# Strided Q and K weights, one head selector, and Q weights loaded by row chunks, in a fused attention-plus-GLU block

## Chip, cores, metric

One core of one Trainium2 chip. The metric is the device time of one execution, in microseconds (us). The kernel before takes 289.22 us (median of four runs, 289.21 to 289.25).

## The reference, cut to what matters

```python
x = A_x                       # 1 x 2048 x 640
xn = _layernorm(x)
# A: attention, 32 heads of 20 features; each position sees itself and 7 positions behind it, 2 apart
qkv = (xn @ wqkv).reshape(B, S, 3, 32, 20)
logits = einsum("bhsd,bhswd->bhsw", q, k[idx]) * 20 ** -0.5     # idx = pos - 2*w, w = 0..7
o = einsum("bhsw,bhswd->bhsd", softmax(masked logits), v[idx])
# B: bilinear GLU
out = x + o @ wo + ((xn @ w_gate) * (xn @ w_up)) @ w_down
```

A head has 20 features, and the 640 features lie on 5 chunks of 128 partitions. So in the natural order some heads straddle chunks: head 6 is features 120 to 139.

## The kernel before

Every operation is recorded in program order by a small scheduler, which inserts the semaphore waits. Everything is bf16 with fp32 accumulation. The work runs in this order: layer norm of 16 row tiles, transposes, Q/K projections; Q*K products on VectorE (DVE) with logits summed per head on TensorE (PE); softmax on DVE; V windows read back from a DRAM scratch, weighted on DVE and summed on PE. The V and GLU projections and the output projection fill PE in between.

Set-up of the head selector, and the first loads:

```python
G = sb("G", [128, NCH, H])                       # one selector for each of 5 chunks
op("pool", memset(G[:], 0.0))
op("pool", affine_select(G[:], G[:], pattern=[[128, NCH], [-DH, H]], compare_op=is_gt,
                         fill=1.0, base=-(DH - 1), channel_multiplier=1))
op("pool", affine_select(G[:], G[:], pattern=[[128, NCH], [-DH, H]], compare_op=is_ge, fill=0.0, ...))
# ... (abridged calls)
def wqkv_load(g, lo=0, hi=D):
    dst = WQKV[:, g, :, lo:hi]
    dma(dst, wqkv_src[:, :, g * D + lo:g * D + hi], ...)

x_load(0)
x_load(1)
wqkv_load(0, 0, 2 * 128)        # Q, columns for output chunks 0 and 1
wqkv_load(0, 2 * 128, D)        # Q, the other columns
x_load(2)
wqkv_load(1)                    # K
for t in range(3, 8):
    x_load(t)
```

The Q/K projections come in three sizes: `proj_part` moves 128 columns of the transposed activations per matmul, `proj_wide` 256 and `proj` 512. All take their weights (the stationary operand) as

```python
l, x = WQKV[:, which, c, m * 128:(m + 1) * 128], XNT[:, c, ...]
```

and every matmul brings its own weight load (PEld in the profile). The logits:

```python
def qk_logits(batch):
    for w, c, s in batch:
        lb = 4 + w % 4
        for j in range(NJ):
            o, x = PS[32 * j:32 * j + 32, lb, :], PRD[:, s, j * JB:(j + 1) * JB]
            matmul(o, G[:, c, :], x, start=(c == 0), stop=(c == NCH - 1), tile_position=(0, 32 * j))
```

The tail adds the residual x, read a second time into XR, and those reads are queued as an item of PE's filling work, behind V windows:

```python
fill.append((0.0, lambda: [xr_load(t) for t in range(NXR)]))     # NXR = 3
add_dn(0)
# ... and, long before that item's turn:
for u in range(NVX):
    vx_load(u)                                                   # first 8 V windows
```

Of the kernel before, what the change touches and what calls it, by code (L numbers as in the profile page):

```python
# [6 lines left out]
ALU = mybir.AluOpType  # L7

S = 2048
D = 640  # L10
NCH = 5
H = 32
DH = 20
# [7 lines left out]
TS = 128  # L21
JB = 512
# [15 lines left out]
class Sched:  # L38
# [47 lines left out]
    def op(self, eng, fn, r=(), w=(), dma=False, name=""):  # L86
        X = _Op()
        X.eng, X.fn, X.name, X.dma = eng, fn, name, dma
        X.needs_tick, X.event, X.pre_know, X.idx = False, None, None, len(self.ops)
        rk = [k for a in r for k in self.keys(a)]  # L90
        wk = [k for a in w for k in self.keys(a)]
        deps = {}
        inorder = eng in ("pe", "act", "dve")
        for k in rk:
            st = self.state.get(k)
            if st is not None and st[0] is not None:
                deps[st[0].idx] = st[0]
        for k in wk:
            st = self.state.get(k)
            if st is None:  # L100
                continue
            o, rds = st
            if o is not None and not (eng == "pe" and o.eng == "pe"):
                deps[o.idx] = o
            for q in rds:
                if inorder and q.eng == eng and not q.dma:
                    continue
                deps[q.idx] = q
        last = {}
        keep = []  # L110
        for d in deps.values():
            if d.dma or d.eng == "pool":
                keep.append(d)
            else:
                b = last.get(d.eng)
                if b is None or b.idx < d.idx:
                    last[d.eng] = d
        X.deps = keep + list(last.values())
        for d in X.deps:
            if not d.dma:  # L120
                d.needs_tick = True
        for k in rk:
            st = self.state.get(k)
            if st is None:
                self.state[k] = [None, [X]]
            elif inorder and st[1] and st[1][-1].eng == eng and not st[1][-1].dma:
                st[1][-1] = X
            else:
                st[1].append(X)
        for k in wk:  # L130
            self.state[k] = [X, []]
        if dma:
            X.event = (self.nc.alloc_semaphore(f"dma{self.n_dma}"), 16)
            self.n_dma += 1
        self.ops.append(X)
        return X
# [59 lines left out]
def build_kernel(nc, A_x, A_wqkv, A_wo, B_x, B_w_gate, B_w_up, B_w_down, out):  # L196
    K = Sched(nc)
    op = K.op
# [3 lines left out]
    def sb(name, shape, dtype=BF16, at=None):  # L202
        n = mybir.dt.size(dtype)
        for s in shape[1:]:
            n *= s
        n = (n + 63) // 64 * 64
        if at is None:
            at = place[0]
            place[0] += n
        assert at + n <= 229344, (name, at + n)  # L210
        return K.sbuf(name, shape, dtype, at)
# [5 lines left out]
    XNT = sb("XNT", [128, NCH, S])  # L217
# [11 lines left out]
    WQKV = sb("WQKV", [128, 3, NCH, D], at=a_ra)  # L229
# [27 lines left out]
    EPSC = sb("EPSC", [128, 16], FP32)  # L257
    IDENT = sb("IDENT", [128, 128])
    SEL = sb("SEL", [128, 32])
    G = sb("G", [128, NCH, H])  # L260
    PS = nc.alloc_psum_tensor("PS", [128, 8, 512], FP32)
    VSL = S + PAD + 2
    vscr = nc.dram_tensor("v_scratch", [4, D, VSL], BF16, kind="Internal").ap()
# [4 lines left out]
    def dma(o, i, r=(), w=(), name="", eng="sp"):  # L268
        return op(eng, lambda e: e.dma_start(o, i), r=r, w=w, dma=True, name=name)  # L269
# [6 lines left out]
                                         fill=1.0, base=0, channel_multiplier=1),  # L276
       r=[IDENT[:]], w=[IDENT[:]], name="ident")
    op("pool", lambda e: e.memset(G[:], 0.0), w=[G[:]], name="g0")
    op("pool", lambda e: e.affine_select(G[:], G[:], pattern=[[128, NCH], [-DH, H]], compare_op=ALU.is_gt,
                                         fill=1.0, base=-(DH - 1), channel_multiplier=1),  # L280
       r=[G[:]], w=[G[:]], name="g1")
    op("pool", lambda e: e.affine_select(G[:], G[:], pattern=[[128, NCH], [-DH, H]], compare_op=ALU.is_ge,
                                         fill=0.0, base=0, channel_multiplier=1),
       r=[G[:]], w=[G[:]], name="g2")
    op("pool", lambda e: e.memset(KT[:, :, 0:PAD], 0.0), w=[KT[:, :, 0:PAD]], name="kpad")

    def x_load(t):
        dma(XST[:, t % NXS, :], xhbm[t * TS:(t + 1) * TS, :], w=[XST[:, t % NXS, :]], name=f"xld{t}")

    wqkv_src = A_wqkv.rearrange("(c p) n -> p c n", p=128)  # L290

    def wqkv_load(g, lo=0, hi=D):
        dst = WQKV[:, g, :, lo:hi]
        dma(dst, wqkv_src[:, :, g * D + lo:g * D + hi], w=[dst], name=f"ld_wqkv{g}_{lo}")

    x_load(0)
    x_load(1)
    wqkv_load(0, 0, 2 * 128)
    wqkv_load(0, 2 * 128, D)
    x_load(2)  # L300
    wqkv_load(1)
    for t in range(3, 8):
# [68 lines left out]
               r=[ZERO[:]], w=[PS[:, 5, :]], name="warm")  # L371


    bank_ring = list(range(6))

    def bank():
        b = bank_ring.pop(0)
        bank_ring.append(b)
        return b

    def proj(which, m, j):
        b = bank()
        for c in range(NCH):
            l, x = WQKV[:, which, c, m * 128:(m + 1) * 128], XNT[:, c, j * JB:(j + 1) * JB]
            op("pe", (lambda l, x, c: lambda e: e.matmul(PS[:, b, :], l, x, start=(c == 0), stop=(c == NCH - 1)))(l, x, c),  # L385
               r=[l, x], w=[PS[:, b, :]], name=f"p{which}_{m}_{j}_{c}")
        T = (QT, KT, VST)[which]
        o0 = PAD if which == 1 else 0
        o = T[:, m, o0 + j * JB:o0 + (j + 1) * JB]
        op("act", lambda e: e.activation(o, PS[:, b, :], ACT.Copy), r=[PS[:, b, :]], w=[o], name=f"pev{which}_{m}_{j}")  # L390

    def proj_part(which, t, ms, b, col):
        for m in ms:
            o = PS[:, b, col + (m - ms[0]) * TS:col + (m - ms[0] + 1) * TS]
            for c in range(NCH):
                l, x = WQKV[:, which, c, m * 128:(m + 1) * 128], XNT[:, c, t * TS:(t + 1) * TS]
                op("pe", (lambda o, l, x, c: lambda e: e.matmul(o, l, x, start=(c == 0), stop=(c == NCH - 1)))(o, l, x, c),  # L397
                   r=[l, x], w=[o], name=f"pp{which}_{m}_{t}_{c}")

    def proj_wide(which, t0, m, b, col):  # L400
        o = PS[:, b, col:col + 2 * TS]
        for c in range(NCH):
            l, x = WQKV[:, which, c, m * 128:(m + 1) * 128], XNT[:, c, t0 * TS:(t0 + 2) * TS]
            op("pe", (lambda l, x, c: lambda e: e.matmul(o, l, x, start=(c == 0), stop=(c == NCH - 1)))(l, x, c),  # L404
               r=[l, x], w=[o], name=f"pw{which}_{m}_{t0}_{c}")

# [20 lines left out]
    def slot_of(w):  # L427
        return (w + 4) % 8
# [6 lines left out]
    def qk_logits(batch):  # L435
        for w, c, s in batch:
            lb = 4 + w % 4
            for j in range(NJ):
                o, x = PS[32 * j:32 * j + 32, lb, :], PRD[:, s, j * JB:(j + 1) * JB]
                op("pe", (lambda o, x, j, c: lambda e: e.matmul(o, G[:, c, :], x, start=(c == 0), stop=(c == NCH - 1),  # L440
                                                             tile_position=(0, 32 * j)))(o, x, j, c),
                   r=[G[:, c, :], x], w=[o], name=f"lg{w}_{c}_{j}")
        for w, c, s in batch:
            if c == NCH - 1:
                lb = 4 + w % 4
                o = LOG[:, slot_of(w), :]
                op("act", (lambda o, lb: lambda e: e.activation(o, PS[:, lb, :], ACT.Copy, scale=SCALE))(o, lb),
                   r=[PS[:, lb, :]], w=[o], name=f"lgev{w}")
                if w > 0:
                    m = LOG[0:32, slot_of(w), 0:DIL * w]  # L450
                    op("pool", (lambda m: lambda e: e.memset(m, NEG))(m), w=[m], name=f"mask{w}")
# [167 lines left out]
    for t0 in (0, 2):  # L619
        bm = bank()  # L620
        for which in (0, 1):
            for t in (t0, t0 + 1):
                b = bank()
                proj_part(which, t, (0, 1), b, 0)
                if (which, t) in ((0, 0), (1, 0), (1, 1), (1, 2), (0, 3)):
                    tr()
                proj_part(which, t, (2, 3), b, 2 * TS)
                part_evac(which, t, 1, 0, 4, b, 0)
                proj_part(which, t, (4,), bm, (2 * which + t - t0) * TS)
            part_evac(which, t0, 2, 4, 1, bm, 2 * which * TS)  # L630
    v_pad()
    for t0 in (4, 6, 8, 10):
        bm = None
        for g in range(5):
# [6 lines left out]
            else:  # L641
                which, m = ((0, 0), (0, 2), None, (1, 0), (1, 2))[g]
# [15 lines left out]
    fill = []  # L658
# [131 lines left out]
```

## Time and profile before

| what | value | view |
|---|---|---|
| time | 289.22 us | median of 4 runs |
| span, PE busy | 287.3 us, 275.4 us (96%) | page, part 1 |
| Q/K weight loads | 450: 200 under 128 moving columns, 200 under 256, 50 under 512 | program, groups |
| pitch of those matmuls (start to start) | 56, 109, 220 ns (216 with every record) | chain, time divided by count |

Part 1 of the page of the kernel before (busy us, share of the span, instructions):

```profile
span 287.3 us, 4706 instructions
PE 275.4 (96%) x1968; PEld 156.7 (55%) x1986; DVE 171.4 (60%) x260; ACT 116.1 (40%) x211; POOL 2.3 (1%) x17
```

PE is the bottleneck, with about 12 us idle in all. The weight loads overlap matmuls, so their 55% is not added to PE's 96%.

The table by stretches of the kernel before. The columns are the stretch, its length, then busy us and instruction count of PE, PEld, DVE, ACT and POOL, the granted clock (the share of full TensorE clock that was let through), the DMA share and GB/s:

```profile
6.37:21.90 15.53, 13.37 (x225) 12.51 (x225) 11.27 (x37) 6.55 (x16) 0.00 (x0) 1.00 0.53 178
...
125.00:178.00 53.00, 49.42 (x368) 24.78 (x369) 48.65 (x42) 19.40 (x36) 0.00 (x0) 0.97 0.58 171
```

PE idles mainly at the start (1.6 us before the first row, 2.2 us in it), in the V stage (3.6 us of the second, where DVE is nearly as busy as PE) and in the 2.8 us after its last matmul.

The chain of work that ended last, kernel before (start us, length us, what; "x40" counts merged instructions):

```profile
3.87 6.92 DMA XST<-in_A_x_dram
10.81 0.50 DVE STATS L327
...
19.91 2.23 PE PS L397 x40
...
23.51 2.18 PE PS L404 x20
...
47.53 8.58 PE PS L385 x39
56.11 0.98 PE PS L440 x16
...
150.47 3.91 DMA XR<-in_A_x_dram
```

Dividing gives the pitches: 2.23/40 = 56 ns with 128 moving columns (L397), 2.18/20 = 109 ns with 256 (L404), 8.58/39 = 220 ns with 512 (L385). Page part 1 has 1968 matmuls but 1986 loads, so 18 matmul records are missing from this trace, one of them here. Two DMAs stand on the chain: x tile 3, landing at about 10.8 us, and the first residual loads, issued at 150.5 us.

Weight loads of the kernel before, grouped with shapes kept apart (count, busy us, mean ns of one, idle before them):

```profile
L404 PEld LDWEIGHTS PS<-XNT,WQKV 128*128 128x128 bf16 x200 | 19.1, 98 | 2.0
L397 PEld LDWEIGHTS PS<-XNT,WQKV 128*128 128x128 bf16 x200 | 11.4, 98 | 1.8 <-DVE XNT L366 1.0 <-ACT KT L412 0.9
L440 PEld LDWEIGHTS PS<-PRD,G 128*32 128x32 bf16 x160 | 3.3, 95 | 6.4 <-DVE PRD L432 2.1 <-issue 1.7 <-ACT VST L390 0.4
L370 PEld LDWEIGHTS PS<-ZERO 128*128 128x128 bf16 x12 | 1.4, 129 | 3.3 <-issue 2.0 <-DVE EPSC L273 1.3
```

A record of one load lasts 98 ns, yet the matmuls follow each other every 56 ns: loads are pipelined, and a record's length is not the time for which it blocks the next. The twelve warm-up matmuls (L370) use one and the same tile and still have twelve loads.

### The profile page before, as it was taken

Reading aid. Unit: us, or ns where it says so; the run is one execution under the profiler, and the core shown is the slowest. Engines: PE = TensorE matmul, PEld = TensorE weight load, DVE = VectorE, ACT = ScalarE, POOL = GpSimd, SP = SyncE. Lnnn points to the kernel's source line nnn. Section 1 sums busy time; section 2 is a strip of 40 time slices with the busy share of each in tenths; the row PEclk is TensorE's granted clock in tenths of the full one; section 3 lists DMA queues with packets and bytes.
Section 4 is the critical chain, followed back from the end, with each engine's and each line's share of the span. In section 5 each row is a group of like instructions: output and inputs, shape, how many; then the busy total and the mean of one; then the engine's idle time right before and its main releaser. Section 6 shows DMA issues by size and latency. Waiting matters only on the chain.

```text
span 287.3 us, 4706 instructions
## 1 busy us (share of the span) xinstructions
PE 275.4 (96%) x1968; PEld 156.7 (55%) x1986; DVE 171.4 (60%) x260; ACT 116.1 (40%) x211; POOL 2.3 (1%) x17
## 2 busy tenths in 40 slices
PE   7899999999999999998997999999999999999996
PEld 3789887443434344443453564444676444677774
DVE  5776792999999768859994999521222112222221
ACT  2355556544644479525732034655200555300000
POOL 2000000000000000000000000000000000000000
PEclk9999999999999999999999799999999999999999
DMA  6824999007989692035976731000021100012211
GB/s 199 281 72 66 396 389 256 3 2 302 392 335 391 217 356 65 0 76 140 307 221 190 208 105 50 2 0 0 2 91 48 46 0 0 2 63 73 74 43 46
DMA packets 30468, 39.57 MB, mean 138 GB/s; under 512 B 4464, under 2 KB 26608, under 8 KB 30448
## 3 DMA queue, kind: packets, MB, share of 16 engines
q1 hardware_dynamic: 30448, 39.29, 41.5%
q8 instruction: 15, 0.25, 0.3%
q14 instruction: 5, 0.04, 0.0%
HBM read 25.07 MB, written 13.16 MB: 133 GB/s over the span
## 4 chain that ended last, share of the span: by engine, by line
PE 72%; DVE 15%; DMA 4%; issue 4%; ACT 2%; SPq 2%; DVEq 0%; ACTq 0%
PE PS L550 27%; PE PS L576 19%; PE PS L385 11%; PE PS L404 7%; PE PS L440 3%; DVE PC L510 3%; DVE PB L510 3%; DMA XST<-in_A_x_dram 2%; PE PS L397 2%; DVE PA L510 2%; SPq L269 2%; DVE SM L455 2%; DMA XR<-in_A_x_dram 1%; PE PS L360 1%; DVE RS L468 1%
## 5 line engine op out<-in xcount | busy, mean ns | idle before, releaser
L550 PE MATMUL PS<-XNT,WU 128*128 128x512 bf16 x238 | 59.4, 379 | 1.4 <-ACT USX L552 1.2
L576 PE MATMUL PS<-WD,HT 128*128 128x320 bf16 x384 | 59.0, 304 | 0.0
L550 PE MATMUL PS<-XNT,WG 128*128 128x512 bf16 x229 | 57.5, 379 | 0.7 <-issue 0.5
L432 DVE TENSOR_TENSOR PRD<-QT,KT 128x2048 bf16<-128x2048 bf16 x40 | 45.8, 1220 | 5.0 <-ACT KT L390 4.2
L576 PEld LDWEIGHTS PS<-WD,HT 128*128 128x128 bf16 x384 | 37.8, 99 | 17.2 <-issue 1.7
L552 ACT ACTIVATE HT<-PS 128x512 bf16<-128x512 f32 x48 | 29.1, 605 | 39.6 <-PE PS L550 39.6
L580 DVE TENSOR_TENSOR FOUT<-PS,XR 128x320 bf16<-128x320 f32 x32 | 15.4, 490 | 46.2 <-PE PS L576 42.5
L555 DVE TENSOR_TENSOR HT<-HT,USX 128x512 bf16<-128x512 bf16 x48 | 19.1, 420 | 39.5 <-ACT USX L552 39.5
L550 PEld LDWEIGHTS PS<-XNT,WU 128*128 128x128 bf16 x240 | 23.3, 98 | 30.1 <-ACT USX L552 1.7
L552 ACT ACTIVATE USX<-PS 128x512 bf16<-128x512 f32 x48 | 28.9, 603 | 26.3 <-PE PS L550 18.3
L550 PEld LDWEIGHTS PS<-XNT,WG 128*128 128x128 bf16 x240 | 22.9, 98 | 29.5 <-issue 1.7
L385 PE MATMUL PS<-XNT,WQKV 128*128 128x512 bf16 x145 | 32.8, 379 | 0.4 <-issue 0.3
L576 PE MATMUL PS<-WO,OT 128*128 128x320 bf16 x160 | 27.1, 300 | 0.0
L385 PEld LDWEIGHTS PS<-XNT,WQKV 128*128 128x128 bf16 x150 | 14.1, 98 | 18.8 <-ACT VST L390 2.1
L404 PE MATMUL PS<-XNT,WQKV 128*128 128x256 bf16 x200 | 23.6, 273 | 0.0
L404 PEld LDWEIGHTS PS<-XNT,WQKV 128*128 128x128 bf16 x200 | 19.1, 98 | 2.0
L527 ACT ACTIVATE OT<-PS 128x512 bf16<-128x512 f32 x20 | 11.1, 600 | 22.3 <-PE PS L520 22.1
L576 PEld LDWEIGHTS PS<-WO,OT 128*128 128x128 bf16 x160 | 15.8, 99 | 6.3
L510 DVE TENSOR_TENSOR PA<-VX,ATX 128x4096 bf16<-128x4096 bf16 x7 | 16.0, 2285 | 4.0 <-DMA ATX<-LOG 4.0
L390 ACT ACTIVATE VST<-PS 128x512 bf16<-128x512 f32 x20 | 12.0, 599 | 14.3 <-PE PS L385 14.3
L510 DVE TENSOR_TENSOR PB<-VX,ATX 128x4096 bf16<-128x4096 bf16 x7 | 16.0, 2285 | 0.2 <-PE PS L520 0.2
L510 DVE TENSOR_TENSOR PC<-VX,ATX 128x4096 bf16<-128x4096 bf16 x6 | 13.7, 2285 | 0.2 <-PE PS L520 0.2
(52 smaller groups left out, 166.5 us busy)
## 6 DMA issues: line engine op xcount, KB each, us to landing
VX<-v_scratch SPq DMA_DIRECT2D x20, 520.0 KB, 5.0
v_scratch<-VST SPq DMA_DIRECT2D x20, 512.0 KB, 4.5
XST<-in_A_x_dram SPq DMA_DIRECT2D x16, 160.0 KB, 4.6
XR<-in_A_x_dram SPq DMA_DIRECT2D x16, 160.0 KB, 2.4
out_dram<-FOUT SPq DMA_DIRECT2D x16, 160.0 KB, 1.8
WG<-in_B_w_gate_dram SPq DMA_DIRECT2D x1, 1920.0 KB, 12.0
WU<-in_B_w_up_dram SPq DMA_DIRECT2D x1, 1920.0 KB, 16.4
WD<-in_B_w_down_dram SPq DMA_DIRECT2D x1, 1920.0 KB, 22.6
```

What stands on the lines that cost most here:

```text
L385: op("pe", (lambda l, x, c: lambda e: e.matmul(PS[:, b, :], l, x, start=(c == 0), stop=(c == NCH - 1)))(l, x, c), r=[l, x], w=[PS[:, b, :] ...
L390: op("act", lambda e: e.activation(o, PS[:, b, :], ACT.Copy), r=[PS[:, b, :]], w=[o], name=f"pev{which}_{m}_{j}")
L404: op("pe", (lambda l, x, c: lambda e: e.matmul(o, l, x, start=(c == 0), stop=(c == NCH - 1)))(l, x, c), r=[l, x], w=[o], name=f"pw{which}_ ...
L432: op("dve", lambda e: e.tensor_tensor(PRD[:, s, :], QT[:, c, :], k, ALU.mult), r=[QT[:, c, :], k], w=[PRD[:, s, :]], name=f"prod{w}_{c}")
L440: op("pe", (lambda o, x, j, c: lambda e: e.matmul(o, G[:, c, :], x, start=(c == 0), stop=(c == NCH - 1), tile_position=(0, 32 * j)))(o, x, ...
L510: op("dve", lambda e: e.tensor_tensor(p[:], vw, a, ALU.mult), r=[v, at], w=[p[:]], name=f"pv{u}")
L527: op("act", (lambda o, b: lambda e: e.activation(o, PS[:, b, :], ACT.Copy))(o, b), r=[PS[:, b, :]], w=[o], name=f"oev{u}")
L550: op("pe", (lambda l, x, c: lambda e: e.matmul(PS[:, b, :], l, x, start=(c == 0), stop=(c == NCH - 1)))(l, x, c), r=[l, x], w=[PS[:, b, :] ...
L552: op("act", lambda e: e.activation(o, PS[:, b, :], ACT.Copy), r=[PS[:, b, :]], w=[o], name=f"guev{which}_{m}_{j}")
L555: h_pending.append(lambda: op("dve", lambda e: e.tensor_tensor(h, h, o, ALU.mult), r=[h, o], w=[h], name=f"h{m}_{j}"))
L576: op("pe", (lambda l, x, i: lambda e: e.matmul(PS[:, b, 0:DHALF], l, x, start=(i == 0), stop=(i == n - 1)))(l, x, i), r=[l, x], w=[PS[:, b ...
L580: op("dve", lambda e: e.tensor_tensor(o, PS[:, b, 0:DHALF], xr, ALU.add), r=[PS[:, b, :], xr], w=[o], name=f"fin{t}_{nb}")
```

## The change

The intent is to reorder the features of Q and K so that every chunk holds the heads alike. Output chunk m takes columns m, m+5, m+10, ... of the weight matrix, so partition p of chunk m is feature 5p+m, which belongs to head p//4 whatever m is. A logit is a sum over a head's features, so the order does not matter as long as Q and K agree. One selector then serves all chunks. Since every output chunk now needs columns from the whole row, Q's weights are loaded by rows of the contraction (chunks 0 to 2, then 3 and 4) instead of by columns.

```diff
-    G = sb("G", [128, NCH, H])
+    G = sb("G", [128, H])
...
-    affine_select(G[:], G[:], pattern=[[128, NCH], [-DH, H]], ..., base=-(DH - 1), ...)
+    affine_select(G[:], G[:], pattern=[[-4, H]], ..., base=-3, ...)
...
-    def wqkv_load(g, lo=0, hi=D):
-        dst = WQKV[:, g, :, lo:hi]
+    def wqkv_load(g, lo=0, hi=NCH):
+        dst = WQKV[:, g, lo:hi, :]
...
-    wqkv_load(0, 0, 2 * 128)
-    wqkv_load(0, 2 * 128, D)
+    wqkv_load(0, 0, 3)
+    wqkv_load(0, 3, NCH)
...
+    def wcols(which, c, m):
+        if which == 2:                                    # V keeps its order
+            return WQKV[:, which, c, m * 128:(m + 1) * 128]
+        return WQKV[:, which, c, m:D:NCH]
...
-            l, x = WQKV[:, which, c, m * 128:(m + 1) * 128], XNT[...]     # in proj, proj_part, proj_wide
+            l, x = wcols(which, c, m), XNT[...]
...
-                matmul(o, G[:, c, :], x, ...)
+                matmul(o, G[:], x, ...)
```

## The prediction

> **What bounds it now.** The page: PE 275.4 of 287.3 us busy (96%), DVE 60%; the chain of waits is 72% PE. The table by stretches: from 6.4 to 22 us PE is 13.4 of 15.5 us busy, fed by layer norm and first loads (the chain passes an x tile landing at 10.8 us); from 22 to 125 us PE has almost no gap; from 178 us on only PE matters. So PE work added or saved goes nearly whole into the time.
>
> **What the change does.** Feature 5p+m sits on partition p of chunk m, so head p//4 has the same partitions in every chunk, and one selector fits all.
>
> - Removed on PE: nothing. The logits keep 160 matmuls of 128x512, each with its own weight load; the groups show 160 loads, and 12 loads for 12 warm-up matmuls of one and the same tile, so equal weights aren't merged. 16 of them take 0.98 us, before and after.
> - The selector shrinks from 160 to 32 columns: POOL's two selects (0.34 us each) shorten, off the chain (first use after 50 us).
> - Q loads: 640 packets of 512 B (27 ns median) and 640 of 768 B (36 ns) become 640 of 1280 B (55 ns). Estimate: 640 x 8 ns / 16 engines = 0.3 us less queue time, so x may land 0.3 us earlier. Against it, the first Q tile needs both Q loads; the last Q packet ended at 7.0 us and would be wanted at 6.6. PE idled 0.39 us before the transposes at 7.5 us anyway: a stall of 0 to 0.4 us, off the chain.
> - Moved: 450 Q/K weight loads (200 at N=128, 200 at N=256, 50 at N=512) read columns 10 B apart instead of 2. The only real risk. Matmul pitch now, from the chain: 2.23 us/40 = 56 ns, 2.18/20 = 109, 8.58/39 = 220; loads hide under matmuls. If a strided load holds the path Z ns, the estimated cost is 200(Z-56) + 200(Z-109) + 50(Z-220), each where positive.
>
> **How large is Z?** The Trainium skill, "TensorE: Matmul & The Clock Gate", section "Weight-path perf modes", says the fast load takes 128 columns as four chunks of 32, "packed or strided". The trace agrees in part: 128-column loads last 98 ns, 32-column ones 95. "SBUF — State Buffer", section "Door 1", says bf16 can stride up to 8 elements for free within 16-byte lines, though two hits a line are wanted; five gives 1.6. No run shows it yet. Even a doubled load should fit below 56 ns (estimate). If the fast load were lost, the first page's P/1.2 gives 107 ns: an estimate of 200 x 51 ns = +10 us (+3.5%). Z = 85 ns would be the 2% line.
>
> **Predicted: 289.4 us, 8 in 10 between 288.4 and 299.** Faster by over 2%: 0.02; within 2%: 0.78; slower: 0.20.
>
> **What would show each step.** Right: pitch at N=128 still 56 ns, at N=256 109; PE busy near 275 us; logits 16 in 0.98 us with 160 loads; the stretch up to 22 us within 0.5 us. Wrong: N=128 pitch over 60 ns or longer Q/K load records (strided reads cost); PE waiting on the second Q load near 6.6 us for over 0.5 us; fewer or faster logits loads; x tiles over 0.5 us sooner.
>
> **What would make it wrong.** Strided columns slowing the load beyond 56 ns, above all beyond 109, when the N=256 part pays too; or a start shifted by the new load order that layer norm doesn't absorb.

## More of the kernel before

Waits of the kernel before in the V stage (who waited for whom: us in total, times, longest):

```profile
DVE FOUT L580 <- DMA XR<-in_A_x_dram: 3.8, 1, 3.8
PE PS L520 <- DVE PA L510: 1.9, 1, 1.9
```

## The result, and the profile after

The changed kernel takes 288.94 us (median of 4 runs, 288.22 to 289.60), against 289.22 us: the same. Ratios here and below are those of fast runs, and are not quite the ratio of the medians. A run counts as slow when it is over 1.5% above the fastest of the same kernel; no timed run here was (experiments 8 and 9 have one run each, and only their traces are used). This ratio is 0.9993, with a 95% interval of 0.9974 to 1.0012.

Page of the changed kernel (its lines from L370 on are numbered up to five higher than before):

```profile
span 287.9 us, 4706 instructions
PE 275.4 (96%) x1968; PEld 159.8 (56%) x1986; DVE 171.4 (60%) x260; ACT 116.1 (40%) x211; POOL 2.0 (1%) x17
```

PE's busy time is the same to the last digit, though both traces lack 18 matmul records; the complete ones of experiments 2 (contiguous weights) and 3 (strided) have 276.4 and 276.2 us. PEld has grown by 3.1 us. The weight loads, with shapes kept apart, show where (L402 answers to L397 before, L409 to L404, L445 to L440):

```profile
L409 PEld LDWEIGHTS PS<-XNT,WQKV 128*128 128x128 bf16 x200 | 21.3, 117 | 0.0
L402 PEld LDWEIGHTS PS<-XNT,WQKV 128*128 128x128 bf16 x200 | 11.6, 118 | 2.2 <-ACT KT L417 0.8 <-DVE MV L339 0.6 <-DMA WQKV<-in_A_wqkv_dram 0.6
L445 PEld LDWEIGHTS PS<-PRD,G 128*32 128x32 bf16 x160 | 3.3, 95 | 6.4 <-DVE PRD L437 2.1 <-issue 1.7 <-ACT VST L395 0.4
```

A strided load's record is 20 ns longer (117 and 118 ns against 98). The logits still have 160 loads. Chain of the changed kernel, the pieces that answer to those above:

```profile
3.71 6.61 DMA XST<-in_A_x_dram
10.34 0.49 DVE STATS L327
...
19.45 2.23 PE PS L402 x40
...
23.06 2.18 PE PS L409 x20
...
47.08 8.58 PE PS L390 x39
55.66 0.98 PE PS L445 x16
...
150.03 4.96 DMA XR<-in_A_x_dram
```

All the pitches are those of before, to the digit: 56, 109 and 220 ns (again with one record missing), and 16 logits matmuls in 0.98 us. Two things differ. Everything from 10 to 150 us happens 0.45 us earlier, because x tile 3 was there earlier. And at 150 us the residual load took 4.96 us instead of 3.91, so that the lead is lost and the span ends 0.6 us later. The waits of the changed kernel say the same:

```profile
DVE FOUT L585 <- DMA XR<-in_A_x_dram: 4.8, 1, 4.8
PE PS L525 <- DVE PA L515: 3.0, 1, 3.0
```

This gives three questions. Is the earlier start part of the change? Do the strided loads cost anything that something else pays back? And does the residual load in the middle blur what can be seen?

### The profile page after: what moved, and what is told of

It reads as the page before. It is cut to its first block, busy times and chain, and to the rows that moved or that the text cites. A ratio compares the mean times of both kernels' runs of the same rounds, so it can differ in the third digit from the quotient of the medians.

```text
span 287.9 us, 4706 instructions
## 1 busy us (share of the span) xinstructions
PE 275.4 (96%) x1968; PEld 159.8 (56%) x1986; DVE 171.4 (60%) x260; ACT 116.1 (40%) x211; POOL 2.0 (1%) x17
## 4 chain that ended last, share of the span: by engine, by line
PE 72%; DVE 16%; DMA 5%; issue 3%; ACT 2%; SPq 2%; DVEq 0%; ACTq 0%
PE PS L555 27%; PE PS L581 19%; PE PS L390 11%; PE PS L409 7%; PE PS L445 3%; DVE PC L515 3%; DVE PA L515 3%; DVE PB L515 3%; DMA XST<-in_A_x_dram 2%; PE PS L402 2%; DMA XR<-in_A_x_dram 2%; DVE SM L460 2%; SPq L269 2%; PE PS L360 1%; DVE RS L473 1%
## 5 line engine op out<-in xcount | busy, mean ns | idle before, releaser
L390 PEld LDWEIGHTS PS<-XNT,WQKV 128*128 128x128 bf16 x150 | 15.1, 105 | 17.9 <-ACT VST L395 2.1
L409 PE MATMUL PS<-XNT,WQKV 128*128 128x256 bf16 x200 | 23.6, 273 | 0.0
L409 PEld LDWEIGHTS PS<-XNT,WQKV 128*128 128x128 bf16 x200 | 21.3, 117 | 0.0
L402 PE MATMUL PS<-XNT,WQKV 128*128 128x128 bf16 x200 | 12.7, 220 | 1.2 <-ACT KT L417 0.7
```

Source lines behind the costliest of these rows:

```text
L390: op("pe", (lambda l, x, c: lambda e: e.matmul(PS[:, b, :], l, x, start=(c == 0), stop=(c == NCH - 1)))(l, x, c), r=[l, x], w=[PS[:, b, :] ...
L402: op("pe", (lambda o, l, x, c: lambda e: e.matmul(o, l, x, start=(c == 0), stop=(c == NCH - 1)))(o, l, x, c), r=[l, x], w=[o], name=f"pp{w ...
L409: op("pe", (lambda l, x, c: lambda e: e.matmul(o, l, x, start=(c == 0), stop=(c == NCH - 1)))(l, x, c), r=[l, x], w=[o], name=f"pw{which}_ ...
```

## The experiments

Theory A: strided loads are longer but hidden, the selector changes nothing, the row loads bring x about 0.45 us sooner, and the residual load gives a varying part of that back. Its rivals are stated with each run. The first four runs shared one chip and 11 runs of the kernel before (288.78 us, 288.10 to 289.43). The next four shared a second chip (before 289.26 us, 288.76 to 289.58), the last four a third (before 288.87 us, 288.32 to 289.23).

### 1. The changed kernel again

No edit.

> The changed kernel again, for its spread. Theory A (the start is 0.45 us earlier, and the first residual load, which landed 3.9 us after its issue before and 5.0 us after the change, gives back a variable part of it): times spread over about 288.2 to 289.7 us again, the first projection at N=512 starts near 47.1 us, and what the profile shows beyond 150 us follows the landing time of that residual load. Rival B (the change is exactly neutral and the spread was chance): times within 0.1 us of 289.2.

Measured: 288.97 us (288.18 to 289.64, 6 runs), ratio 1.0005 (0.9988 to 1.0023). The spread came as Theory A said, and not as Rival B's 0.1 us, but the kernel before spreads as widely on this chip. The earlier start did not come back: statistics of x tile 3 began at 11.21 us, and the projections with 512 columns at 47.73 us, later than in the kernel before. So Theory A's 0.45 us, read from one pair of traces, was at least mostly the chance of one load's landing. That part of the theory fell. The other part held: the residual load was issued at 150.9 us, took 4.0 us, and set the rest. In all seven profiles with the late residual load (the two above, experiments 1 to 3, 6 and 7) the span ends 132.78 or 132.79 us after the first residual addition begins: in the kernel before, 154.47 + 132.79 = 287.26 us.

### 2. Only the row loads

```diff
 (kernel before)
-    wqkv_load(0, 0, 2 * 128)
-    wqkv_load(0, 2 * 128, D)
+    wqkv_load(0, 0, 3)          # with the changed wqkv_load
+    wqkv_load(0, 3, NCH)
```

> Only the Q loads by row chunks, with contiguous weights and five selectors as before. Theory A (the earlier start comes from the fewer DMA packets): x tile of the chain lands near 10.3 us instead of 10.8, the N=512 projections start near 47.1 us as with the whole change, Q/K load records stay at 98 ns, time 288.2 to 289.7 us as with the change. Rival C (the earlier start comes from the shorter selector set-up or the strided reads): start near 47.5 us, time 289.2.

Measured: 288.89 us (288.48 to 290.01, 6 runs), ratio 1.0005 (0.9987 to 1.0023). Records stay at 98 ns, as expected. Tile 3's statistics began at 10.61 us and the 512-column projections at 47.11 us:

```profile
10.61 0.50 DVE L327 BATCH_NORM_STATS2 STATS<-XST 128x6 f32<-128x320 bf16 x1 [1.26 <-DMA XST<-in_A_x_dram]
...
47.11 1.67 PE L385 MATMUL PS<-XNT,WQKV 128*128 128x512 bf16 x7
```

The second is Theory A's figure and the first lies between the theories; with landings that scatter as in experiment 1, one trace decides neither.

### 3. Only the stride and the selector

```diff
 (changed kernel)
-    wqkv_load(0, 0, 3)
-    wqkv_load(0, 3, NCH)
+    wqkv_load(0, 0, 2 * 128)    # with the earlier wqkv_load, by columns
+    wqkv_load(0, 2 * 128, D)
```

> Strided weights and one selector, Q loaded by column blocks as before. Theory A: the Q/K load records are 117 ns as with the whole change, pitch stays 56/109/220 ns, x lands near 10.8 us, N=512 projections start at 47.5 us (up to 0.4 us later if the wait for the second Q load isn't absorbed), time 289.2 +- 0.3 us. Rival C: start near 47.1 us. Rival D (strided reads cost time that the loads gave back): start later than 48 us and time over 290 us.

Measured: 288.89 us (288.55 to 289.07, 6 runs), ratio 1.0000 (0.9987 to 1.0013). Records are 117 ns and the start of the 512-column projections is 47.59 us, so Rival D (a cost hidden by a gain) is out at this precision. The traces say it more sharply than the times. Here are the same two events as in experiment 2:

```profile
11.07 0.49 DVE L327 BATCH_NORM_STATS2 STATS<-XST 128x6 f32<-128x320 bf16 x1 [1.10 <-DMA XST<-in_A_x_dram]
...
47.59 1.24 PE L390 MATMUL PS<-XNT,WQKV 128*128 128x512 bf16 x5
```

From the statistics of tile 3 to the first 512-column projection it is 36.52 us with strided weights, here and in experiment 1, and 36.50 us with contiguous ones in experiment 2. (The two traces above give 36.72 and 36.74 us, because the first of these matmuls is the missing record.) When tile 3 lands varies; what follows does not. This run also shows what the row loads are for. Timeline of PE in this run, first Q projections (start, busy us, ..., idle before and what ended it):

```profile
8.22 0.73 PE L402 MATMUL PS<-XNT,WQKV 128*128 128x128 bf16 x10 [1.30 <-DVE XNS L349]
```

The first projection starts at 8.22 us, against 6.53 us in the changed kernel, whose timeline is

```profile
6.53 0.34 PE L402 MATMUL PS<-XNT,WQKV 128*128 128x128 bf16 x3 [0.15 <-DMA WQKV<-in_A_wqkv_dram]
...
7.27 0.58 PE L402 MATMUL PS<-XNT,WQKV 128*128 128x128 bf16 x7 [0.41 <-DMA WQKV<-in_A_wqkv_dram]
```

With row loads three matmuls can go as soon as the first rows are there, and the other chunks are waited for only 0.41 us. With column loads and strided columns nothing can start until both blocks have landed: in this run the last packet of Q ended at 7.8 us. (The view puts the wait down to DVE, but the activations were copied at 6.06 to 6.55 us; where the named engine had long been done, it was another, here the load.) Yet the delay of 1.7 us is gone by 47.6 us, because the chain there runs through x tile 3.

### 4. Residual loads moved forward, in the changed kernel

The reads of the first three residual tiles go out before the first V windows, from 90.9 us on in the trace, instead of at 150 us.

```diff
-    fill.append((0.0, lambda: [xr_load(t) for t in range(NXR)]))
...
+    for t in range(NXR):
+        xr_load(t)
     for u in range(NVX):
         vx_load(u)
```

> The changed kernel with the first three residual loads issued ahead of the first V windows (near 95 us) instead of at 150 us. Theory A: DVE no longer waits about 4.8 us for the residual at 150 us; PE idled only 3.0 us behind it, so the time falls by about 3 us to 286.0 to 286.8 us, and the spread shrinks below 0.3 us. Rival B: the residual load isn't on the chain, time 288.9 us with the same spread.

Measured: 285.83 us (285.50 to 286.12, 5 runs), ratio 0.9894 (0.9878 to 0.9911). Right in size (2.95 us), though just below the 286.0 to 286.8 us expected; the spread is 0.6 us, not under 0.3, against 1.3 us of the kernel before. The waits of PE in this run no longer hold the wait on the DVE product of the first buffer, and DVE has no wait for the residual. What is left there is

```profile
PE PS L525 <- DVE PC L515: 0.9, 1, 0.9
```

This gain belongs to neither version of the weights. It shows that the wait at 150 us was on the chain: the first residual addition begins at 150.59 us, and the rest takes 133.69 us. The drop in the granted clock that some runs show (see the last section) is not what was gained, since runs of the kernel before without it took 288.58 to 288.79 us on this chip. The edit also makes a quieter base for comparing.

### 5. Residual loads moved forward, in the kernel before

Edit as in 4.

> The kernel before with the first three residual loads issued ahead of the first V windows. If the change itself is neutral (records of strided loads longer but hidden, selectors unmerged, start within the spread of the load landings): 285.5 to 286.3 us, the same as the changed kernel with this edit (285.83), DVE's wait of 3.8 us for the residual gone. If the change has a small cost or gain that the residual wait covered: a difference of over 0.5 us from 285.83.

Measured: 286.36 us (286.08 to 286.63, 4 runs), ratio 0.9899 (0.9884 to 0.9914) to the kernel before on this chip. The median is 0.53 us above that of experiment 4, so by the letter of the expectation (over 0.5 us, and above 286.3) it points to a small gain from the change; but the chip is another one, and in its profile tile 3's statistics began at 11.37 us against 10.72 us in experiment 4's. The ratios, each to the kernel before on its own chip, agree to 0.05%. Experiment 10 repeats the pair on one chip.

### 6. A stride at which every column has its own 16-byte line

Its output is wrong, which doesn't matter for the time.

```diff
-        return WQKV[:, which, c, m:D:NCH]
+        flat = WQKV[:, which].rearrange("p c n -> p (c n)")
+        return flat[:, c * NCH + m:NCH * D:NCH * NCH]        # stride 25: 50 B
```

> Wrong result on purpose: the Q and K weights of the changed kernel read at a column stride of 25 (50 B) over the five chunks instead of 5 (10 B), so that every column lies in a 16-byte line of its own; same loads, same matmuls. If the longer record of a strided load (117 ns against 98) comes from crossing 16-byte lines: the record grows clearly beyond 117 ns; as long as a load holds the path under 56 ns, the pitch at N=128 stays 56 ns and the time 288.2 to 289.7 us; if it holds it longer, the pitch at N=128 rises above 60 ns and the time over 290 us. If any stride over one costs the same: record 117 ns, time unchanged.

Measured: 290.14 us (290.02 to 290.46, 5 runs), ratio 1.0034 (1.0021 to 1.0046), relative error 1.13. This is the one weight stride that cost time. Weight loads of this run, with shapes kept apart:

```profile
L410 PEld LDWEIGHTS PS<-XNT,WQKV 128*128 128x128 bf16 x200 | 21.8, 146 | 0.0
...
L403 PEld LDWEIGHTS PS<-XNT,WQKV 128*128 128x128 bf16 x200 | 13.9, 157 | 1.7 <-DVE SD L348 1.0 <-ACT KT L418 0.8
```

and two pieces of its chain:

```profile
20.46 2.68 PE PS L403 x40
...
24.52 2.19 PE PS L410 x20
```

The pitch with 128 moving columns is 2.68/40 = 67 ns instead of 56, with 256 columns 2.19/20 = 110 ns, practically unchanged. By the prediction's formula Z = 67 ns gives 200 x 11 ns = 2.2 us; 0.34% of 289.26 us is 1.0 us. The trace shows more directly what reached the chain: from the statistics of tile 3 (10.46 us) to the first 512-column projection (48.41 us) it is 37.95 us, 1.4 us more than at stride 5. That the rest fell before tile 3, where PE waits anyway, is likely but was not measured by itself. The 1.0 us also holds the chance of tile 3's landing, and depends on what is compared: experiment 7's kernel, on the same chip and with stride 5, has a median 1.7 us lower.

### 7. One selector stored five times

```diff
 (changed kernel)
-    G = sb("G", [128, H])
+    G = sb("G", [128, NCH, H])      # five equal copies, pattern=[[0, NCH], [-4, H]]
-                matmul(o, G[:], x, ...)
+                matmul(o, G[:, c, :], x, ...)
```

> The changed kernel with the one selector stored five times and read by chunk, as before: tests the part 'one head selector' alone. Theory A (equal weights aren't merged, the selector's set-up is off the chain): 160 loads for the logits in both, 16 logits matmuls in 0.98 us, time 288.2 to 289.7 us. Rival: sharing one selector saves PE time, then this one is slower by over 0.5 us than the changed kernel.

Measured: 288.48 us (4 runs: 288.30, 288.35, 288.61 and one of 291.53), ratio 1.0000 (0.9958 to 1.0042); 160 logits loads of 95 ns in both. Sharing a selector saves PE no load. The single long run was not explained (its mean granted clock was 0.988); it makes this interval the widest, 1.2 us either way, so the time alone could not show the 0.5 us of the rival. The count of loads and the 0.98 us do.

### 8. The load path by itself

After the changed kernel's work, groups of 64 matmuls were added, each with its own weight load, moving only 32 columns (the last three groups 128), so that a matmul cannot hide a load.

```diff
+    def bench(fn, name):
+        for k in range(64):
+            op("pe", fn, r=[XNT[:, 0, :]], w=[PS[:, 0, :]], name=name)
+    bench(lambda e: e.matmul(PS[0:128, 0, 0:32], XNT[:, 0, 0:128:1], XNT[:, 1, 0:32], ...))   # L764, stride 1
+    bench(lambda e: e.matmul(PS[0:128, 0, 0:32], XNT[:, 0, 0:256:2], ...))                    # L765, stride 2
+    ...  # L766 4, L767 5, L768 8, L769 12, L770 16; L771 to L773: 32 weight columns at 1, 5, 16
```

> The changed kernel, then groups of 64 matmuls with their own weight load each, moving only 32 columns (three last groups 128), weights of 128 columns at a stride of 1, 2, 4, 5, 8, 12, 16, of 32 columns at 1, 5, 16. The pitch of a group shows how long a load holds the path when no matmul hides it. Theory A: stride 1 at 25 to 40 ns, stride 5 longer by up to the 20 ns that its record is longer, so 45 to 56 ns, hidden under 56; strides from 8 (16 B) on longer still. With 128 moving columns stride 1 and 5 both at 56 ns, stride 16 perhaps more. Rival (the longer record is only latency): the same pitch for all strides.

Timeline of PE in this run (start us, time from the first start to the last end, line, shape of the weights, shape of what moves):

```profile
284.32 1.75 PE L764 MATMUL PS<-XNT 128*128 128x32 bf16 x64
285.92 1.75 PE L765 MATMUL PS<-XNT 128*128 128x32 bf16 x64
287.52 2.29 PE L766 MATMUL PS<-XNT 128*128 128x32 bf16 x64
289.67 2.71 PE L767 MATMUL PS<-XNT 128*128 128x32 bf16 x64
292.22 4.02 PE L768 MATMUL PS<-XNT 128*128 128x32 bf16 x64
...
303.88 1.89 PE L771 MATMUL PS<-XNT 128*32 128x32 bf16 x64
305.61 2.71 PE L772 MATMUL PS<-XNT 128*32 128x32 bf16 x64
308.17 4.11 PE L773 MATMUL PS<-XNT 128*32 128x32 bf16 x64
```

The pitch of a group is the next group's start minus its own, over 64. Stride 1 (L764): (285.92 - 284.32)/64 = 25 ns; stride 4 (L766): 34 ns; stride 5 (L767): (292.22 - 289.67)/64 = 40 ns. With 32 weight columns instead of 128, stride 1 takes 27 ns (L771) and stride 5 again 40 ns (L772). So a strided load does hold the path longer, by 15 ns or more (stride 1 may be shorter than the 25 ns at which these small matmuls follow each other anyway), and it stays below 56 ns. The rival (only latency) is out. The expectation of 45 to 56 ns was a little high. From stride 8 on, most groups of this run ran at a granted clock of 0.5 to 0.8, so experiment 9 repeats strides of 8 and more at a higher clock.

### 9. The load path again, with the clock kept up

As experiment 8, with 24 matmuls of 512 columns before each group; strides 3, 6, 7, 8, 25 with 32 moving columns, then 5 and 25 with 128, and 25 with 256.

> The changed kernel, then groups of 64 small matmuls as in the first such run, each after 24 matmuls of 512 columns that keep the clock up. Theory E (a load of 128 columns holds the path for about 2 ns for each 16-byte line that 32 of its columns touch, at least the 25 ns floor of a small matmul): stride 3 at 25 to 28 ns, 6 at 48, 7 at 56, 8 at 61 to 64, 25 at 64; moving 128 columns, stride 5 at 56 and stride 25 at 64; moving 256 columns, stride 25 at 109. Rival (the cost grows with the stride itself): stride 25 well over stride 8.

Timeline of PE in this run, for stride 8 (L777) and 25 (L779) with 32 moving columns and 25 with 128 (L783); a line L764 here is the 24 matmuls between two groups:

```profile
315.41 3.98 PE L777 MATMUL PS<-XNT 128*128 128x32 bf16 x64
319.23 6.86 PE L764 MATMUL PS<-XNT 128*128 128x512 bf16 x24
325.93 4.39 PE L779 MATMUL PS<-XNT 128*128 128x32 bf16 x64
330.15 6.52 PE L764 MATMUL PS<-XNT 128*128 128x512 bf16 x24
...
345.26 4.42 PE L783 MATMUL PS<-XNT 128*128 128x128 bf16 x64
349.52 5.34 PE L764 MATMUL PS<-XNT 128*128 128x512 bf16 x24
```

| weight stride, columns | bytes | 16-byte lines that 32 columns touch | pitch, 32 moving | pitch, 128 moving |
|---|---|---|---|---|
| 1 | 2 | 4 | 25 (exp. 8) | 56 (kernel before) |
| 3 | 6 | 12 | 27 | |
| 4 | 8 | 16 | 34 (exp. 8) | |
| 5 | 10 | 20 | 40 (exp. 8) | 56 |
| 6 | 12 | 24 | 46 | |
| 7 | 14 | 28 | 53 | |
| 8 | 16 | 32 | 60 | |
| 25 | 50 | 32 | 66 | 67 |

The pitches are in ns and from this run where nothing else is said; for example stride 8 is (319.23 - 315.41)/64 = 60. The granted clock was 0.96 in the group of stride 8, 0.88 in that of 25 with 32 moving columns, and 1.0 in the rest of this run's. The clock hardly mattered to such a group: stride 8 took 60 ns at 0.59 in experiment 8 as well.

Above the floor of 25 to 27 ns the pitch is close to 2 ns for each line touched, and it nearly stops growing once every column has its own line: going from stride 8 to 25 triples the step and adds 6 ns, where going from 4 to 8 adds 26. The rival (cost grows with the stride itself) is out as the main cause. Theory E's 64 ns for stride 25 was 2 to 3 ns low, and its figures for strides 6, 7 and 8 were 1 to 4 ns high, so the rule is good to about 10%, and its mechanism is inferred from the sizes. With 256 moving columns, stride 25 kept a median pitch of 109 ns.

### 10. The pair again on one chip, and one more step

> The kernel before with early residual loads again, on the same chip as the next one: with the wait that varied most taken out of both, the change can be seen to about 0.2%. If the change is neutral: within 0.5 us of the next one.

> The changed kernel with early residual loads again. Neutral change: within 0.5 us of the one above, about 286 us. A real gain of the fewer packets (estimate 0.3 us) would show as 0.2 to 0.4 us less than the one above.

Measured: 286.06 us (285.72 to 286.16, 5 runs), ratio 0.9902 (0.9889 to 0.9916), with the weights of before; 285.86 us (285.69 to 286.02, 4 runs), ratio 0.9896 (0.9883 to 0.9910), with the changed ones. The intervals overlap, and the 512-column projections started at 47.22 and 47.24 us. The medians differ by 0.2 us, the lower edge of what a real gain was expected to show. A gain of this size from the change is not excluded and not shown. It could come only from the start: from tile 3's statistics to the end of the span it is 273.53 us in both traces with the weights of before (this one and experiment 5's), and 273.56 and 273.59 us in the two with the changed ones.

Last, x tile 3 before the K weights, on top of the changed kernel with early residual loads:

```diff
     x_load(2)
+    x_load(3)
     wqkv_load(1)
-    for t in range(3, 8):
+    for t in range(4, 8):
         x_load(t)
```

> The same with the load of x tile 3 issued before that of the K weights instead of behind it. If the start's chain waits for x tile 3 behind 800 KB of K weights: bn_stats of tile 3 starts 1 to 2 us sooner than 10.3 to 11.4 us, the N=512 projections start 0.3 to 1 us sooner, and the time falls by as much, to about 285.2 us, unless PE then waits for K.

Measured: 285.28 us (285.07 to 285.42, 4 runs), ratio 0.9876 (0.9862 to 0.9889): the fastest version, 0.6 us below experiment 4's kernel on the same chip. Statistics of tile 3 began at 8.87 us instead of 10.71, the 512-column projections at 46.45 us instead of 47.24. Its chain shows what took over:

```profile
3.71 6.96 DMA WQKV<-in_A_wqkv_dram
...
10.71 0.75 PE PS L403 x10
```

PE now waits for K's weights at the start of the chain, as the expectation feared, but only after a net gain.

## Why the prediction was right

- **PE bound, nothing removed on it.** Right. PE's busy time is 275.4 us before and after, with 160 logits loads and 0.98 us for 16 logits matmuls in both. Experiment 7 shows that five copies of the selector change neither.
- **The strided load is the only risk, and it stays hidden.** Right, and measured: Z is 40 ns at a stride of five, under the 56 ns of the shortest matmul, so each of the three terms of the sum is zero; from tile 3's statistics to the 512-column projections it is 36.5 us with either weights. The 20 ns longer record, which the prediction listed as a sign of cost, is no such sign: the record grew and the pitch did not. Record and pitch have to be read together.
- **The threshold is real.** Right: a stride of 25 holds the path for 67 ns. Then the 128-column matmuls slow to 67 ns, and the 256-column ones don't. Of the formula's 2.2 us, 1.4 us reached the chain behind tile 3, and about 1.0 us the time.
- **The fast load survives a stride.** The Trainium skill, "TensorE: Matmul & The Clock Gate", section "Weight-path perf modes", has it taking four chunks of 32 columns "packed or strided". Experiment 8 agrees: 128 columns cost what 32 cost, 40 ns at stride 5 and 62 to 64 ns at stride 16 (there at a granted clock of 0.5 and 0.7). The fallback of 107 ns for a lost fast load did not arise.
- **The free stride.** The prediction leant on "SBUF — State Buffer", section "Door 1", for bf16 strides of up to 8 being free. Here the measurement differs: nothing was free on the load path from stride 4 on. The prediction came out right because the cost was hidden, not because it was absent. What held was its sum, which charges a load only above 56 ns. To that extent it was lucky: at a stride of 8, which the same passage also calls free, the pitch is 60 ns.
- **The start.** The estimate of 0.3 us from fewer packets is not settled. Over all profiles but the last step's, tile 3's statistics began at 10.81, 11.07, 11.37 and 10.72 us with column loads, and at 10.34, 11.21, 10.61, 10.46, 10.16, 10.72, 10.71, 10.26 and 11.65 us with row loads (the last two are experiments 8 and 9). The means, 10.99 and 10.68 us, differ by the estimate, but single landings scatter by up to 1.5 us. The wait for the second Q load was 0.41 us and off the chain, as predicted.

My first reading of the result was wrong, though: a 0.45 us lead taken from one pair of traces as a property of the change. The second trace of the same kernel had no lead.

## What to carry to other kernels

In these runs a weight load cost time only when it held the load path for longer than the matmul that hides it (40 ns under 56 cost nothing, 67 ns did), so compare its pitch, measured where nothing hides it, with the matmul pitch, and not its record. Strided weight columns are then a cheap way to permute features, as long as the moving operand is long enough; and a permutation that only makes operands equal saves nothing where each matmul loads its weights anyway (160 loads with one selector as with five). When a change is neutral to within the spread, look for the waits that make the spread: here, in the profiles, two DMA landings set it, x tile 3's and the residual's (from the statistics of tile 3 to the issue of the residual load it is 139.64 to 139.70 us wherever that load is late and the stride is one or five). Moving the second was worth 1%, while the change was worth nothing measurable.

## What the Trainium skill lacked or had wrong

- "TensorE: Matmul & The Clock Gate", "Weight-path perf modes": no cost is given for strided columns in a fast load. Here the pitch is 25 ns at stride 1 and 2, 27 at 3, 34 at 4, 40 at 5, 46 at 6, 53 at 7, 60 at 8 and 66 to 67 at 25 (bf16), the same for 32 and 128 columns at strides 5 and 16.
- The same page, "LDWEIGHTS (loading the stationary operand)": columns over 1.2 would be 107 ns for 128 columns, with no word there of the fast load that the page describes after it. Here 128 contiguous bf16 columns take at most the 25 to 27 ns that 32 take.
- The same page, "Back-to-back issue gap": it gives about 81 ns for a stream of load and matmul pairs with 128 moving columns. Here it is 56 ns, with every load contiguous or at stride 5, as in its formula without loads.
- "SBUF — State Buffer", "Door 1": eight bf16 as a stride that is free. On the weight-load path a stride of 4 already takes 34 ns against 25, and 8 takes 60.
- The first page again, "The HAM clock gate": it has the clock halved after an idle window of about 3.4 us. In the kernel before, one wait of PE of 1.95 us, ending at 157.6 us, was followed by a window at a granted clock of 0.5 (158.6 to 161.5 us); in the two profiles of experiments 2 and 3 waits of 1.7 and 1.8 us were not, and in that of experiment 8 one of 2.5 us was not either. The drop did not lengthen the rest: 132.79 us follow the first residual addition with it and without. A run with this drop has a mean granted clock of 0.994. With the residual loads moved forward the mean was 0.999 or 1.0 in all 22 runs. What decides is open.
